# Work moved from VectorE to GpSimd in attention, one multiplication where there were two, and a new order: attention followed by two expert layers on one core

## The chip, the cores and the metric

One core of a Trainium2 chip runs the whole kernel. The metric is device time in microseconds, the median of several executions. Below, TensorE is also PE (its weight loads PEld), VectorE DVE, ScalarE ACT, GpSimd POOL, and the queue that issues most transfers SP.

## The reference

Three stages follow one another, all in fp32:

```
attention: 2 batches x 8 heads, 576 rows, 64 columns a head; x 1152 rows of 512
  scores = q k^T / 8 + (cum[i] - cum[j]), causal;  cum = cumsum(log(clip(f)))
  p = exp(scores - rowmax);  out = (p / (sum(p) + 1e-9)) @ v
layer 1: each row goes to argmax(x @ w_gate + modality_bias[modality_id]) of 8 experts
  out = gate * relu(x w1[e]) w2[e]        (512 -> 1024 -> 512)
layer 2: the same with other weights and no bias; an expert takes at most 288 rows
```

## The kernel before

**Precision by pairs.** Operands of the large matrix products are split into a high part (rounded to fp32r) and a low part (the value less the high part). ACT writes high parts, DVE most low parts. For the weights this is `chunk` (line 364 the high half on ACT, line 373 the low half on DVE), each weight chunk of 128x1024 in two halves of 512 columns.

**A head of attention.** Keys and queries are turned on PE (lines 535, 574, 595) and split (K: L543 on ACT, L547 on DVE, a copy L561 on POOL; Q: L608, L612, L623 likewise; V: L632 on ACT, low part L643 on POOL). Four extra rows, with the cumulated logarithms of f, come from DRAM by a transfer that POOL issues (L1123). Scores are two matmuls and a mask (L675, L676, L679) for each of five tiles of query rows; DVE takes the row maxima (L689), ACT the exponentials with their row sums into `st` (L697). PE turns the exponentials (L715), ACT and DVE split them (L722, L726), and PE multiplies them with V (L748). ACT brings the result to SBUF (L760, L764), and L772 multiplies it with `iw`, which gives for each row 64 output columns and 8 gate logits, side by side in PSUM (72 = NCX columns).

**The end of a head** is what the change touches. On DVE: 1e-9 is added to the row sums (L777) and the reciprocal taken (L780); L785 multiplies the 64 columns by it into `xs`, L789 the 8 logits into `lgh`. After the seventh head of a batch L797 and L800 add the logits of seven heads and the bias, after the eighth L804 adds the last. After each second head SP writes two heads' columns to DRAM (L811 for 512 rows, with 512 bytes a row; L815 for the last 64 rows).

**What follows attention.** While batch 1 is in attention, `early` finds the rows of batch 0 that go to the first expert (L963 to L1019, some thirty small DVE operations in a chain), POOL gathers them (L1025), and the first of that expert's matmuls (`hidden`, L1068) are put between the last heads. For these the first four weight chunks must be split during attention: eight halves, L364 and L373. The buffer that a chunk came in is then loaded with a later chunk (L371, SP).

**What sets the order.** Each operation is handed to a planner (`Sched`) with an engine, an assumed duration and a priority: head number times T plus an offset by kind (`off` in `PAR`; 'N' is the end of a head). The planner writes each engine's fixed program order. Engines take their instructions strictly in that order, so one that waits holds back all behind it on its engine. The split of chunk m has priority (wsp + wsd * m) * T.

Of the kernel before, what the change touches and what calls it, by code (L numbers as in the profile page):

```python
# [8 lines left out]
F32 = mybir.dt.float32  # L9
# [4 lines left out]
ALU = mybir.AluOpType  # L14
AX = mybir.AxisListType
# [3 lines left out]
P = 128  # L19
# [214 lines left out]
def kernel(  # L234
# [17 lines left out]
    par=None,  # L252
):
    nc = tc.nc
    B, H, S, D = q.shape
    N, DM = out.shape
    E = wg1.shape[1]
    BH = B * H
# [18 lines left out]
    psum = actx.enter_context(tc.tile_pool(name="psum", bufs=1, space=PSUM))  # L277

    c_ql_, c_kl_, c_vl_ = ([at.take(sh, F32) for _ in range(n)] for n, sh in ((3, [P, NT, 2, D]), (2, [P, NT, 2, D]), (2, [P, NT, 2, D])))
    iw, xs_ = at.take([P, H, NCX], F32), at.take([P, NT, DM], F32)  # L280
    lf = xs_[0:BH, 0:2].rearrange("p a b -> p (a b)")[:, 0:S]
    nc.sync.dma_start(out=lf, in_=f.rearrange("b h s -> (b h) s"))

    def rows(src, h):
# [60 lines left out]
    def chunk(m, e=None, src=None, raw=None):  # L345

        i, c = divmod(m, NCH)
        rt = RAW[m % NR if raw is None else raw]
        if e is None:
            e, src = expert_of(i)  # L350
        hi, lo = SPL[m % NS] if m % NS < len(SPL) else (None, None)
        if c < KD:
            rv, sv = rt, pick(src[0], e)[c * P:(c + 1) * P, :]
        else:
            k0 = 2 * (c - KD)
            rv = rt.rearrange("p (a d) -> p a d", d=DM)
            sv = pick(src[1], e)[k0 * P:(k0 + 2) * P, :].rearrange("(a p) d -> p a d", p=P)

        def half(t, u):
            return t[:, u * (F1 // 2):(u + 1) * (F1 // 2)]  # L360

        def high(u, eng=None):
            if eng is None:
                nc.scalar.copy(out=half(hi, u), in_=half(rt, u))  # L364
            else:
                eng.tensor_tensor(
                    out=half(hi, u), in0=half(rt, u), in1=one_c.to_broadcast([P, F1 // 2]), op=ALU.mult
                )

        return (  # L370
            lambda: nc.sync.dma_start(out=rv, in_=sv),  # L371
            high,
            lambda u, eng: eng.tensor_tensor(out=half(lo, u), in0=half(rt, u), in1=half(hi, u), op=ALU.subtract),  # L373
        )
# [103 lines left out]
    for t in fresh("ot"):  # L478
        nc.gpsimd.memset(t[:, S:NT * P], 0.0)
    c_rs = slots("rs", [P, NT, 1], F32, 2)  # L480
    lgh = [at.take([P, NT, H, E], F32)] * B
    c_xs = sc.cls("xs", [xs_])

    if not par.get("only"):
# [38 lines left out]
    def head(h, L, G):  # L523
# [243 lines left out]
        def zo():  # L767
            return z.ap[:, HQ:HQ + NT * NCX].rearrange("p (i c) -> p i c", c=NCX)
# [5 lines left out]
        rs = Buf(c_rs)  # L774

        def fn():
            nc.vector.tensor_tensor(  # L777
                out=rs.ap[:, :, 0], in0=st.ap, in1=eps_c.to_broadcast([P, NT]), op=ALU.add
            )
            nc.vector.reciprocal(out=rs.ap, in_=rs.ap)  # L780
        sc.op(D_, 0.17, fn, r=[st], w=[rs], prio=base + O["N"])
        xs = G["xs", b]

        def fn():
            nc.vector.tensor_tensor(  # L785
                out=xs.ap[:, :, hh * D:(hh + 1) * D], in0=zo()[:, :, 0:D],
                in1=rs.ap.to_broadcast([P, NT, D]), op=ALU.mult,
            )
            nc.vector.tensor_tensor(  # L789
                out=lgh[b][:, :, hh, :], in0=zo()[:, :, D:NCX],  # L790
                in1=rs.ap.to_broadcast([P, NT, E]), op=ALU.mult,
            )
        sc.op(D_, 0.5, fn, r=[z, rs], w=[xs, G["lgh"]], prio=base + O["N"])
        lgb = lg[:, 0:E, b * NT:(b + 1) * NT]
        if hh == H - 2:
            def fn():
                nc.vector.tensor_reduce(  # L797
                    out=lgb, in_=lgh[b][:, :, 0:H - 1, :].rearrange("p i h e -> p e i h"), axis=AX.X, op=ALU.add
                )
                nc.vector.tensor_tensor(out=lgb, in0=lgb, in1=btok[:, :, b * NT:(b + 1) * NT], op=ALU.add)  # L800
            sc.op(D_, 0.6, fn, r=[G["lgh"]], w=[G["lg"]], prio=base + O["N"], after=[G["c6"]])
        if hh == H - 1:
            def fn():
                nc.vector.tensor_tensor(  # L804
                    out=lgb, in0=lgb, in1=lgh[b][:, :, H - 1, :].rearrange("p i e -> p e i"), op=ALU.add
                )
            sc.op(D_, 0.12, fn, r=[G["lgh"]], w=[G["lg"]], prio=base + O["N"])
        if hh % 2 == 1:
            def fn():
                c0, t0 = (hh - 1) * D, b * S  # L810
                nc.sync.dma_start(  # L811
                    out=x_d[t0:t0 + KC * P, c0:c0 + 2 * D].rearrange("(i p) d -> p i d", p=P),
                    in_=xs.ap[:, 0:KC, c0:c0 + 2 * D],
                )
                nc.sync.dma_start(  # L815
                    out=x_d[t0 + KC * P:t0 + S, c0:c0 + 2 * D], in_=xs.ap[0:KR, KC, c0:c0 + 2 * D]
                )
            n_ = sc.op("SP", 1.0, fn, r=[xs], prio=base + O["N"], dma=0.83)
            if b == 0:
                G["x0"].append(n_)  # L820

# [276 lines left out]

    a5 = sc.op(D_, 0.2, consts5, prio=par["c5"] * T, after=chain(steps5, par["c5"] * T, [a1, a4]), late=1.0)
    (a6,) = chain(steps6, par["c6"] * T, [a3, a5])  # L1100
    G["c6"], G["lg"], G["lgh"] = a6, Buf(None), Buf(None)
    sc.op("SP", 0.5, zfill2, after=[a3], prio=par["zf"] * T, dma=7.0)
    for b in range(B):
        G["xs", b] = Buf(c_xs)
# [29 lines left out]
    for m in range(NR0):  # L1134
        lb, last, wpr = Buf(None), [], (par["wsp"] + par["wsd"] * m) * T
        sc.op(
            "SP", 0.5, lambda m=m: chunk(m)[0](), w=[lb], after=[a5, a8], dma=1.46, prio=par["w0"] + m * par["w1"],
            late=par["wlate"],
        )
        for u in range(2 if m < KD else 0):  # L1140
            hb = Buf(None)
            if 2 * m + u < par["whp"]:
                sc.op("POOL", 1.2, lambda m=m, u=u: chunk(m)[1](u, nc.gpsimd), r=[lb], w=[hb], prio=wpr + 0.1 * u)
            else:
                sc.op(A_, 0.52, lambda m=m, u=u: chunk(m)[1](u), r=[lb], w=[hb], prio=wpr + 0.1 * u)
            last.append(
                sc.op(D_, 0.61, lambda m=m, u=u: chunk(m)[2](u, vec), r=[hb], w=[wsp[m]], prio=wpr + 0.1 * u)
            )
        if m < KD:
            split_ += last  # L1150
            sc.op("SP", 0.5, lambda m=m: chunk(m + NR)[0](), after=last, dma=1.46, fill=True)
# [1192 lines left out]


PAR = dict(
    wsp=10.0, wsd=0.5528,
    q2n=0, qt=2.7571,
    xprio=4.0,
    te=18.0, dur1=5.6, c5=4.0, c6=5.0, pace=(9.0, 42.0, 2.7),  # L2350
# [3 lines left out]
    marg=0.05, glate=4.0, w2p=1.5, k2e='POOL', ve='ACT', T=7.517, window=29.6757,  # L2354
    w0=54.7241, warm=12, qodd=0.8391, vodd=0.4187, w1=3.4882,
    nbig=2, none=4, pt=[[[0, 0, 576], [3, 384, 576], [4, 512, 576]], [[1, 128, 576]], [[2, 256, 576]]],
    kodd=0.9248, groups=[[4], [3], [2], [0, 1]], off={'aug': -19.3748, 'load': -22.0501, 'T': -13.4108, 'E': -23.4736, 'V': -9.7976, 'S': -5.8296, 'M': -8.5396, 'X': -1.2687, 'PT': -5.0955, 'H': -11.8233, 'AV': 1.8376, 'OT': -16.2636, 'O': 19.7458, 'N': -2.4012}, wf0=6.5, wfd=0.6,
)


# [31 lines left out]
```

## Time and profile before

| what | value |
|---|---|
| median of 3 runs | 469.11 us (468.78 to 472.85) |
| profiled execution | 468.58 us, span 466.8 us |
| PE, PEld busy | 433.5 us (93%), 364.5 us (78%) |
| DVE, ACT, POOL busy | 314.9 us (67%), 270.0 us (58%), 132.0 us (28%) |
| attention's last operation on the logits (L804) | starts at 160.60 us |

A recorded duration includes the time in which an instruction's last results drain, so that back-to-back instructions overlap in the record; a matmul's end is modelled. Idle time is what no recorded instruction covers, with what released the instruction after it. Shares for the whole span mix attention (to about 160 us) with the expert layers.

### The profile page before, as it was taken

The page shows a single profiled execution, that of the slowest core. Times are in us where ns is not written, and L with a number is a line of the kernel's source. Part 1 is how long each engine was busy: PE and PEld are TensorE (multiplying, and loading weights), DVE is VectorE, ACT ScalarE, POOL GpSimd, SP SyncE. Part 2 cuts the span into 40 slices and gives each one's busy share as a digit, 9 for nine tenths or more (in the row PEclk, how much of TensorE's full clock was granted, in tenths as well). Part 3 has the DMA queues.
Part 4 walks back from the last instruction along what each step waited for, and adds up shares of the span by engine and source line. Part 5 has one row for each costly group of instructions (what it writes and reads, how often), then busy time and mean ns, then how long its engine had stood idle before and what let it go on. Part 6 is the DMA issues. An engine that isn't in the chain of part 4 may idle for free. (4 is left out here: it accounts for less than half of the span.)

```text
span 466.8 us, 8038 instructions
## 1 busy us (share of the span) xinstructions
PE 433.5 (93%) x2701; PEld 364.5 (78%) x2701; DVE 314.9 (67%) x717; ACT 270.0 (58%) x603; POOL 132.0 (28%) x171
## 2 busy tenths in 40 slices
PE   7899899898899999999999999989999999999970
PEld 6688787787689978988989877768887778778750
DVE  6787998899985687411952146777849997497330
ACT  6778778799676435202831116356848985597130
POOL 8773344363340013101200010151313344111100
PEclk9999999999999999999999999989999999999996
DMA  6563199994310166501560003349666999460000
GB/s 151 78 145 76 30 157 178 289 289 133 96 67 1 53 207 211 182 24 47 190 217 24 23 24 104 134 125 328 229 208 203 305 322 307 133 210 3 32 4 23
DMA packets 64294, 64.91 MB, mean 139 GB/s; under 512 B 37196, under 2 KB 46412, under 8 KB 64224
## 3 DMA queue, kind: packets, MB, share of 16 engines
q1 hardware_dynamic: 58048, 53.89, 39.7%
q0 software_dynamic: 4992, 10.08, 6.9%
q8 instruction: 25, 0.41, 0.4%
q10 hardware_dynamic: 1200, 0.30, 0.3%
q14 instruction: 29, 0.24, 0.2%
HBM read 56.56 MB, written 11.87 MB: 147 GB/s over the span
## 5 line engine op out<-in xcount | busy, mean ns | idle before, releaser
L2259 POOL DMA_INDIRECT out_dram<-mo,mo x16 | 18.6, 1164 | 104.8 <-DVE mo L2252 83.7
L697 ACT ACTIVATE at<-one,at 128x512 f32<-128x512 f32 (+1 forms) x64 | 33.4, 527 | 9.0 <-DVE at L689 8.6
L748 PE MATMUL one<-at,at 128*128 128x64 f32 (+2 forms) x192 | 35.9, 327 | 2.6 <-ACT at L697 1.5
L2183 ACT ACTIVATE mo<-hps 128x512 f32<-128x512 f32 x30 | 17.7, 606 | 31.0 <-PE hps L2170 18.7
L748 PEld LDWEIGHTS one<-at,at 128*128 128x128 f32 x192 | 28.7, 190 | 5.8 <-ACT at L697 2.2
L2219 PE MATMUL yps<-mo,wb 128*128 128x512 f32 x72 | 29.1, 405 | 0.6 <-PEq L2147 0.3
L689 DVE TENSOR_REDUCE at<-one 128x1 f32<-128x512 f32 (+1 forms) x64 | 28.1, 475 | 0.7 <-PE one L679 0.6
L2221 PE MATMUL yps<-mo,wb 128*128 128x512 f32 x72 | 28.5, 396 | 0.0
L2220 PE MATMUL yps<-mo,wb 128*128 128x512 f32 x72 | 28.5, 396 | 0.0
L1424 POOL DMA_INDIRECT x_d<-mo,mo x8 | 8.1, 1018 | 70.8 <-DVE mo L1421 49.7
L715 PE MATMUL big<-ident,at 128*128 128x128 f32 x128 | 24.3, 274 | 3.8 <-DVE at L547 3.8
L373 DVE TENSOR_TENSOR mo<-wa,mo 128x512 fp32r<-128x512 f32 x42 | 27.3, 682 | 0.7 <-ACT mo L364 0.7
L675 PE MATMUL one<-at,at 128*128 128x512 f32 (+1 forms) x64 | 25.8, 404 | 1.5 <-DVE at L726 1.4
L364 ACT CAST mo<-wa 128x512 fp32r<-128x512 f32 x42 | 24.9, 643 | 0.8 <-DMA wb<-in_moe_w_dram 0.8
L2252 DVE TENSOR_SCALAR mo<-yps,mo 128x512 f32<-128x512 f32 x14 | 10.4, 744 | 21.6 <-PE yps L2221 21.6
L373 DVE TENSOR_TENSOR mo<-wb,mo 128x512 fp32r<-128x512 f32 x36 | 23.7, 684 | 0.5 <-ACT mo L364 0.5
L726 DVE TENSOR_TENSOR at<-one,at 128x320 fp32r<-128x320 f32 (+1 forms) x32 | 17.4, 552 | 9.6 <-ACT at L722 9.4
L715 PE MATMUL one<-ident,at 128*128 128x128 f32 x112 | 22.4, 277 | 1.2 <-ACT at L697 0.6
L373 DVE TENSOR_TENSOR wa<-wb,wa 128x512 fp32r<-128x512 f32 x34 | 21.9, 683 | 2.0 <-ACT wa L364 2.0
L1399 ACT COPY mo<-ytps 128x512 f32<-128x512 f32 (+1 forms) x10 | 5.7, 566 | 30.0 <-PE ytps L1392 30.0
L1268 POOL DMA_INDIRECT wb<-x_d,mo x7 | 7.2, 1023 | 53.4 <-DVE wb L1903 35.9
L364 ACT CAST mo<-wb 128x512 fp32r<-128x512 f32 x36 | 21.4, 636 | 0.8 <-PE yps L2221 0.8
(428 smaller groups left out, 1355.6 us busy)
## 6 DMA issues: line engine op xcount, KB each, us to landing
wb<-in_moe_w_dram SPq DMA_DIRECT2D x35, 512.0 KB, 5.3
wa<-in_moe_w_dram SPq DMA_DIRECT2D x31, 512.0 KB, 5.6
mo<-in_moe_w_dram SPq DMA_DIRECT2D x14, 512.0 KB, 4.4
x_d<-zero SPq DMA_DIRECT2D x1, 2340.0 KB, 18.7
at<-in_k_dram SPq DMA_DIRECT2D x16, 128.0 KB, 2.9
at<-in_q_dram SPq DMA_DIRECT2D x16, 128.0 KB, 2.8
at<-in_v_dram SPq DMA_DIRECT2D x16, 128.0 KB, 2.8
x_d<-at SPq DMA_DIRECT2D x8, 256.0 KB, 2.4
```

Source lines behind the costliest of these rows:

```text
L364: nc.scalar.copy(out=half(hi, u), in_=half(rt, u))
L373: lambda u, eng: eng.tensor_tensor(out=half(lo, u), in0=half(rt, u), in1=half(hi, u), op=ALU.subtract),
L675: nc.tensor.matmul(o, q1.ap[:, s0:s0 + n], k1.ap[:, a:e], start=True, stop=False)
L689: nc.vector.tensor_reduce(out=nm.ap[0:n], in_=ps.ap[0:n, c:c + w], axis=AX.X, op=ALU.max, negate=True)
L697: nc.scalar.activation(out=p.ap[0:n, 0:w], in_=ps.ap[0:n, c:c + w], func=AF.Exp, bias=nm.ap[0:n], scale=1.0, accum_out=st.ap[0:n, i:i + 1],)
L715: nc.tensor.transpose(out=t.ap[:, c:c + P], in_=ptile[i].ap[:, j * P:(j + 1) * P], identity=ident)
L748: nc.tensor.matmul(dst.ap[:, qa - off:qb - off], vt.ap[:, j].rearrange("p a d -> p (a d)"), ph[a][u].ap[:, ca:ca + qb - qa], start=(first ...
L2183: nc.scalar.activation(out=self.s.ap[:, 4 * i:4 * i + 4, :], in_=self.h[i].ap.rearrange("p (c t) -> p c t", t=P), func=AF.Relu,)
L2219: nc.tensor.matmul(self.y.ap, a, wh, start=(c == 0), stop=False)
L2220: nc.tensor.matmul(self.y.ap, a, wl, start=False, stop=False)
L2221: nc.tensor.matmul(self.y.ap, b, wh, start=False, stop=(c == KF - 1))
L2259: nc.gpsimd.indirect_dma_start(out=out, out_offset=blk.at(), in_=o.ap[:, 0:DM], in_offset=None, bounds_check=N - 1, oob_is_err=False,)
```

## The change

It does five things. The low parts of the first four weight chunks (eight halves) are computed by POOL instead of DVE, and their priorities spread from 0.5528 to 0.8093 heads a chunk. Adding 1e-9 to the row sums is an operation of POOL of its own, with a priority 2 us ahead of the reciprocal's, which stays on DVE. `xs` holds 72 columns for each head, so one multiplication over 72 columns takes the place of two over 64 and 8, and `lgh` goes. The write to DRAM after two heads becomes three transfers: one for each head's 512 rows (256 bytes a row) and one for the last 64 rows of both. Five offsets of the plan and `kodd` (the split of the odd head's keys) have other values.

```diff
@@ -277,8 +277,8 @@
     psum = actx.enter_context(tc.tile_pool(name="psum", bufs=1, space=PSUM))
 
     c_ql_, c_kl_, c_vl_ = ([at.take(sh, F32) for _ in range(n)] for n, sh in ((3, [P, NT, 2, D]), (2, [P, NT, 2, D]), (2, [P, NT, 2, D])))
-    iw, xs_ = at.take([P, H, NCX], F32), at.take([P, NT, DM], F32)
-    lf = xs_[0:BH, 0:2].rearrange("p a b -> p (a b)")[:, 0:S]
+    iw, xs_ = at.take([P, H, NCX], F32), at.take([P, NT, H, NCX], F32)
+    lf = xs_[0:BH, 0].rearrange("p a b -> p (a b)")[:, 0:S]
     nc.sync.dma_start(out=lf, in_=f.rearrange("b h s -> (b h) s"))
 
     def rows(src, h):
@@ -478,7 +478,6 @@
     for t in fresh("ot"):
         nc.gpsimd.memset(t[:, S:NT * P], 0.0)
     c_rs = slots("rs", [P, NT, 1], F32, 2)
-    lgh = [at.take([P, NT, H, E], F32)] * B
     c_xs = sc.cls("xs", [xs_])
 
     if not par.get("only"):
@@ -774,48 +773,49 @@
         rs = Buf(c_rs)
 
         def fn():
-            nc.vector.tensor_tensor(
+            nc.gpsimd.tensor_tensor(
                 out=rs.ap[:, :, 0], in0=st.ap, in1=eps_c.to_broadcast([P, NT]), op=ALU.add
             )
+        sc.op("POOL", 0.15, fn, r=[st], w=[rs], prio=base + O["N"] - par["rsp"])
+
+        def fn():
             nc.vector.reciprocal(out=rs.ap, in_=rs.ap)
-        sc.op(D_, 0.17, fn, r=[st], w=[rs], prio=base + O["N"])
+        sc.op(D_, 0.12, fn, w=[rs], prio=base + O["N"])
         xs = G["xs", b]
 
         def fn():
             nc.vector.tensor_tensor(
-                out=xs.ap[:, :, hh * D:(hh + 1) * D], in0=zo()[:, :, 0:D],
-                in1=rs.ap.to_broadcast([P, NT, D]), op=ALU.mult,
+                out=xs.ap[:, :, hh, :], in0=zo(), in1=rs.ap.to_broadcast([P, NT, NCX]), op=ALU.mult
             )
-            nc.vector.tensor_tensor(
-                out=lgh[b][:, :, hh, :], in0=zo()[:, :, D:NCX],
-                in1=rs.ap.to_broadcast([P, NT, E]), op=ALU.mult,
-            )
-        sc.op(D_, 0.5, fn, r=[z, rs], w=[xs, G["lgh"]], prio=base + O["N"])
+        sc.op(D_, 0.45, fn, r=[z, rs], w=[xs], prio=base + O["N"])
         lgb = lg[:, 0:E, b * NT:(b + 1) * NT]
         if hh == H - 2:
             def fn():
                 nc.vector.tensor_reduce(
-                    out=lgb, in_=lgh[b][:, :, 0:H - 1, :].rearrange("p i h e -> p e i h"), axis=AX.X, op=ALU.add
+                    out=lgb, in_=xs.ap[:, :, 0:H - 1, D:NCX].rearrange("p i h e -> p e i h"), axis=AX.X, op=ALU.add
                 )
                 nc.vector.tensor_tensor(out=lgb, in0=lgb, in1=btok[:, :, b * NT:(b + 1) * NT], op=ALU.add)
-            sc.op(D_, 0.6, fn, r=[G["lgh"]], w=[G["lg"]], prio=base + O["N"], after=[G["c6"]])
+            sc.op(D_, 0.6, fn, r=[xs], w=[G["lg"]], prio=base + O["N"], after=[G["c6"]])
         if hh == H - 1:
             def fn():
                 nc.vector.tensor_tensor(
-                    out=lgb, in0=lgb, in1=lgh[b][:, :, H - 1, :].rearrange("p i e -> p e i"), op=ALU.add
+                    out=lgb, in0=lgb, in1=xs.ap[:, :, H - 1, D:NCX].rearrange("p i e -> p e i"), op=ALU.add
                 )
-            sc.op(D_, 0.12, fn, r=[G["lgh"]], w=[G["lg"]], prio=base + O["N"])
+            sc.op(D_, 0.12, fn, r=[xs], w=[G["lg"]], prio=base + O["N"])
         if hh % 2 == 1:
             def fn():
                 c0, t0 = (hh - 1) * D, b * S
+                for u in range(2):
+                    c = c0 + u * D
+                    nc.sync.dma_start(
+                        out=x_d[t0:t0 + KC * P, c:c + D].rearrange("(i p) d -> p i d", p=P),
+                        in_=xs.ap[:, 0:KC, hh - 1 + u, 0:D],
+                    )
                 nc.sync.dma_start(
-                    out=x_d[t0:t0 + KC * P, c0:c0 + 2 * D].rearrange("(i p) d -> p i d", p=P),
-                    in_=xs.ap[:, 0:KC, c0:c0 + 2 * D],
+                    out=x_d[t0 + KC * P:t0 + S, c0:c0 + 2 * D].rearrange("p (r d) -> p r d", d=D),
+                    in_=xs.ap[0:KR, KC, hh - 1:hh + 1, 0:D],
                 )
-                nc.sync.dma_start(
-                    out=x_d[t0 + KC * P:t0 + S, c0:c0 + 2 * D], in_=xs.ap[0:KR, KC, c0:c0 + 2 * D]
-                )
-            n_ = sc.op("SP", 1.0, fn, r=[xs], prio=base + O["N"], dma=0.83)
+            n_ = sc.op("SP", 1.6, fn, r=[xs], prio=base + O["N"], dma=1.0)
             if b == 0:
                 G["x0"].append(n_)
 
@@ -1098,7 +1098,7 @@
 
     a5 = sc.op(D_, 0.2, consts5, prio=par["c5"] * T, after=chain(steps5, par["c5"] * T, [a1, a4]), late=1.0)
     (a6,) = chain(steps6, par["c6"] * T, [a3, a5])
-    G["c6"], G["lg"], G["lgh"] = a6, Buf(None), Buf(None)
+    G["c6"], G["lg"] = a6, Buf(None)
     sc.op("SP", 0.5, zfill2, after=[a3], prio=par["zf"] * T, dma=7.0)
     for b in range(B):
         G["xs", b] = Buf(c_xs)
@@ -1144,7 +1144,9 @@
             else:
                 sc.op(A_, 0.52, lambda m=m, u=u: chunk(m)[1](u), r=[lb], w=[hb], prio=wpr + 0.1 * u)
             last.append(
-                sc.op(D_, 0.61, lambda m=m, u=u: chunk(m)[2](u, vec), r=[hb], w=[wsp[m]], prio=wpr + 0.1 * u)
+                sc.op(
+                    "POOL", 1.25, lambda m=m, u=u: chunk(m)[2](u, nc.gpsimd), r=[hb], w=[wsp[m]], prio=wpr + 0.1 * u
+                )
             )
         if m < KD:
             split_ += last
@@ -2344,7 +2346,8 @@
 
 
 PAR = dict(
-    wsp=10.0, wsd=0.5528,
+    rsp=2.0,
+    wsp=10.0, wsd=0.8093,
     q2n=0, qt=2.7571,
     xprio=4.0,
     te=18.0, dur1=5.6, c5=4.0, c6=5.0, pace=(9.0, 42.0, 2.7),
@@ -2354,7 +2357,7 @@
     marg=0.05, glate=4.0, w2p=1.5, k2e='POOL', ve='ACT', T=7.517, window=29.6757,
     w0=54.7241, warm=12, qodd=0.8391, vodd=0.4187, w1=3.4882,
     nbig=2, none=4, pt=[[[0, 0, 576], [3, 384, 576], [4, 512, 576]], [[1, 128, 576]], [[2, 256, 576]]],
-    kodd=0.9248, groups=[[4], [3], [2], [0, 1]], off={'aug': -19.3748, 'load': -22.0501, 'T': -13.4108, 'E': -23.4736, 'V': -9.7976, 'S': -5.8296, 'M': -8.5396, 'X': -1.2687, 'PT': -5.0955, 'H': -11.8233, 'AV': 1.8376, 'OT': -16.2636, 'O': 19.7458, 'N': -2.4012}, wf0=6.5, wfd=0.6,
+    kodd=1.1276, groups=[[4], [3], [2], [0, 1]], off={'aug': -20.7153, 'load': -22.0501, 'T': -14.5461, 'E': -23.4736, 'V': -9.7976, 'S': -5.8296, 'M': -8.8671, 'X': -1.2687, 'PT': -5.5058, 'H': -11.8233, 'AV': 1.8376, 'OT': -16.2636, 'O': 19.7458, 'N': -2.2729}, wf0=6.5, wfd=0.6,
 )
```

## Rows read from the trace of the kernel before

**Rows 1.** Stretches: us, PE, PEld, DVE, ACT, POOL busy (instructions), clock, DMA, GB/s

```profile
20.00:95.00 75.00, 70.34 (x523) 60.49 (x522) 65.47 (x144) 59.50 (x159) 37.42 (x60) 1.00 0.70 143
95.00:126.00 31.00, 27.66 (x206) 22.31 (x203) 30.54 (x79) 25.98 (x66) 12.56 (x15) 1.00 0.55 167
126.00:141.00 15.00, 14.54 (x111) 12.43 (x110) 13.13 (x27) 12.12 (x33) 6.74 (x8) 1.00 0.28 90
141.00:160.00 19.00, 19.00 (x154) 18.22 (x154) 9.65 (x23) 11.53 (x29) 0.00 (x0) 1.00 0.06 18
```

**Rows 2.** Waits of PE, 95 to 126 us: total us, times, longest

```profile
PE one L675 <- DVE at L726: 1.2, 2, 0.7
PE one L748 <- DVE at L789: 1.1, 1, 1.1
PE big L715 <- DVE at L547: 0.5, 1, 0.5
PE one L715 <- DVE wb L1019: 0.3, 1, 0.3
```

**Rows 3.** Waits of PE, 20 to 95 us

```profile
PE big L715 <- DVE at L547: 3.3, 3, 1.4
```

**Rows 4.** DVE's groups, 95 to 126 us: busy, mean ns, idle before

```profile
L373 DVE TENSOR_TENSOR wa<-wa,wa 128x512 fp32r<-128x512 f32 x8 | 5.9, 740 | 0.0
...
L777 DVE TENSOR_TENSOR at<-at,eps_c 128x5 f32<-128x5 f32 x4 | 0.6, 151 | 0.0
```

**Rows 5.** DVE's groups, 0 to 155 us

```profile
L785 DVE TENSOR_TENSOR at<-one,at 128x320 f32<-128x320 f32 x14 | 6.7, 478 | 0.3 <-PE one L772 0.2
...
L777 DVE TENSOR_TENSOR at<-at,eps_c 128x5 f32<-128x5 f32 x16 | 3.8, 238 | 0.8 <-ACT at L697 0.6
...
L789 DVE TENSOR_TENSOR at<-one,at 128x40 f32<-128x40 f32 x14 | 2.6, 183 | 0.0
```

**Rows 6.** POOL's groups, 95 to 126 us

```profile
L561 POOL TENSOR_TENSOR at<-at,one_c 64x576 fp32r<-64x576 f32 x3 | 3.9, 1323 | 1.9 <-ACT at L543 1.9
L623 POOL TENSOR_TENSOR at<-at,one_c 64x576 fp32r<-64x576 f32 x3 | 3.4, 1142 | 2.4 <-ACT at L608 2.4
L643 POOL TENSOR_TENSOR at<-at,at 128x320 fp32r<-128x320 f32 x3 | 2.6, 881 | 3.7 <-ACT at L632 3.7
```

**Rows 7.** Timeline of DVE: start us, us

```profile
51.78 0.62 DVE L777 TENSOR_TENSOR at<-at,eps_c 128x5 f32<-128x5 f32 x1
...
105.35 0.79 DVE L971 SCALAR_TENSOR_TENSOR wb<-wb 128x40 f32<-128x40 f32 x1
...
124.02 0.69 DVE L373 TENSOR_TENSOR wa<-wa,wa 128x512 fp32r<-128x512 f32 x1
```

**Rows 8.** Timeline of POOL: start us, us, idle before and its releaser

```profile
50.13 2.24 POOL L561 TENSOR_TENSOR at<-at,one_c 64x576 fp32r<-64x576 f32 x2 [2.13 <-ACT at L543]
...
105.22 0.86 POOL L643 TENSOR_TENSOR at<-at,at 128x320 fp32r<-128x320 f32 x1 [0.31 <-ACT at L632]
...
171.52 1.04 POOL L1268 DMA_INDIRECT wb<-x_d,mo  x1 [35.86 <-DVE wb L1903]
```

**Rows 9.** Waits of POOL, 0 to 160 us: total us, times, longest

```profile
POOL at L1123 <- PE one L679: 17.1, 6, 3.3
POOL at L643 <- ACT at L632: 12.3, 9, 3.4
...
POOL wb L1025 <- DVE wb L1019: 4.6, 1, 4.6
```

**Rows 10.** Timeline of PE: the first matmul that needs the eight halves

```profile
143.82 1.43 PE L1068 MATMUL big<-wb,wa 128*128 128x256 f32 x10
```

**Rows 11.** Page, DMA issues: KB each, median us to landing

```profile
at<-in_k_dram SPq DMA_DIRECT2D x16, 128.0 KB, 2.9
...
x_d<-at SPq DMA_DIRECT2D x8, 256.0 KB, 2.4
```

**Rows 12.** Timeline of SP at the end of attention: start us, us

```profile
160.90 0.52 SPq L815 DMA_DIRECT2D x_d<-at  x1
```

## The prediction

> **What bounds the kernel now.** I read the stretches first, because the share of the whole span mixes attention with the expert layers. From 95 to 126 us DVE is busy for 30.54 of 31.00 us: there it is the saturated engine, and PE is idle for 31.00 - 27.66 = 3.34 us. From 20 to 95 us DVE has room (65.47 of 75 us) and PE is idle for 4.66 us. From 126 to 141 us PE lacks 0.46 us, from 141 to 160 us nothing at all [rows 1]. So a change that relieves DVE can pay before 126 us, and behind 141 us PE itself is the limit: what comes out of attention earlier moves the rest of the kernel forward by as much, because the expert layers have no instruction of the change in them.
>
> The second view is what PE waited for. From 95 to 126 us it is DVE each time: 1.2 us for low parts of the exponentials, 1.1 us for the logits' multiplication (it frees the PSUM tile), 0.5 us for low parts of K, 0.3 us for the early route, 3.1 us in all of the 3.34 [rows 2]. From 20 to 95 us it is 3.3 us for low parts of K [rows 3]. The reader is to see that 3.1 + 3.3 = 6.4 us is about all that a faster DVE can give back. A little more hides behind the drain that a record includes, so I let the ceiling be 8 us.
>
> **The change part by part: what DVE loses.** The eight low halves take 740 ns each, 8 x 0.740 = 5.9 us, all of it in the saturated stretch [rows 4]. Adding 1e-9 takes 16 x 0.238 = 3.8 us over the span, though only 4 x 0.151 = 0.6 us in the stretch [rows 4, 5]. The second multiplication, 183 ns for 40 columns, becomes 40 more columns of the first. At the first one's 478 / 320 = 1.5 ns a column that is 0.06 us, so each head saves 0.183 - 0.06 = 0.12 us, 16 x 0.12 = 2.0 us over the span and 0.4 us in the stretch (three heads) [rows 5]. Sum: 5.9 + 3.8 + 2.0 = 11.7 us over attention, 5.9 + 0.6 + 0.4 = 6.9 us in the stretch.
>
> **What POOL gains.** The trace has no fp32 subtraction of 512 columns on POOL. The nearest is the low part of V, two inputs from SBUF, 881 ns for 320 columns; in proportion that gives 881 x 512 / 320 = 1.41 us. The other end follows from the slope to the copies of 576 columns (1142 ns): 881 + 192 x (1142 - 881) / 256 = 1.08 us [rows 6]. I take 1.25 us, between the two, since the operation is the nearer one in kind and the width lies between: 8 x 1.25 = 10 us, with 8.6 and 11.3 as ends. Adding 1e-9 to five columns isn't there either: not under DVE's 0.15, not over the 0.88 of 320 columns [rows 4, 6]; I take 0.2, near the short end, 16 x 0.2 = 3.2 us. POOL is busy for 12.56 of 31 us in the stretch [rows 1]; with some 7 us of the halves (the last two chunks are now planned later) and 0.8 us of additions it comes to 20, so it has the time. The halves' consumer is the first early matmul at 143.82 us [rows 10]; the last half now starts at 124.02 us [rows 7]. Chunk 3 is put off by 3 x (0.8093 - 0.5528) = 0.77 heads of about 9 us, to about 131 us, which leaves 11 us of cover. If that cover goes, PE waits at 143.82 for what is missing.
>
> **What the port costs.** POOL and DVE stand in each other's way here: the addition at 51.78 us took 0.62 us where its kind takes 0.15, and ended at 52.40, just when POOL's copies of 50.13 to 52.37 had ended; a small operation of the early route at 105.35 took 0.79 us and ended with POOL's 105.22 to 106.08 [rows 4, 7, 8]. So the change takes victims away (additions, halves) and leaves about ten operations of the early route with two SBUF inputs. POOL's SBUF work covers 3.9 + 3.4 + 2.6 = 9.9 us of the 31, about 0.32 [rows 6]; 7 us more make it 0.55. Ten operations x 0.23 more chance x half of 1.25 us is 1.4 us that DVE gives back. Ends: 0 (none is hit) and 10 x 0.62 = 6.2 us (each is).
>
> **Moved and added waits.** POOL's queue is long on waits: 17.1 us in six waits before the transfers of the four rows, 12.3 us in nine before V's low parts, 4.6 us before the early gather [rows 9]. Whatever stands behind them (the halves, the additions) is late with them, and behind a half of 1.25 us the copies of K and Q and the four rows' transfers start later in turn; they are made about a head ahead, which hides most of it. I charge 0.5 us, with 0 and 3 as ends (a wait of a copy's length, 1.14 us, some three times). The reciprocal now waits for POOL; behind it on DVE stand the next head's maxima and low parts, for which ACT and PE wait. That is the rival below.
>
> **The transfers.** SP issues one transfer more for each pair of heads: 0.4 us, which matters only where something queues behind it. Two of 128 KB with short rows land in about 2.9 us like the loads of K, where 256 KB took 2.4 [rows 11]. The last pair was issued by 160.90 + 0.52 us [rows 12]; landing at 163 it becomes 164 to 164.5. The first reader is the gather at 171.52 us, released by DVE [rows 8]: 7 us of cover, so I cost it at nothing; the ends are 0 and 1 us. The Trainium skill, "DMA: Bandwidth & Descriptors", Specifications, puts the least size for full rate at 512 bytes and has the engines read, modify and write below it, which speaks against this part; by it the sum would still be the same, since the cover is longer than twice the old landing time.
>
> **The sum.** In the stretch DVE is relieved of 6.9 - 1.4 = 5.5 us, more than the 3.1 us that PE waited for it. I take 2.8 of these, because relieved waits partly pass to ACT. Before 95 us DVE loses about 8 x (0.238 + 0.12) = 2.9 us, where it isn't saturated; of the 3.3 us I take a third, 1.1. Less 0.5 for POOL's queue: 2.8 + 1.1 - 0.5 = 3.4 us. The profiled execution took 468.58 us, 0.5 below the median, and would become 465.2; against the median the forecast is 469.11 - 3.4 = **465.7 us**. The new offsets only permute the order; I give them 0, with 2 us either way.
>
> **The rivals.** (a) More comes back: the new order also removes most of the waits on K's low parts (transposes are planned 1.1 us earlier), and the whole 6.4 us and the drains go: -7, 462. For it speaks that these waits are few and long (1.4 us [rows 3]), against it that DVE has room there and they are matters of order. (b) The port takes it back: every one of the ten operations meets a half, 6.2 us, so that 6.9 - 6.2 = 0.7 us is left, time 468.5. The additions and the operation of 105.35 show that the mechanism exists. The Trainium skill, "SBUF — State Buffer", Who interferes with whom, says that a DVE instruction with two SBUF inputs and a GpSimd instruction that reads SBUF exclude each other for the whole instruction; the trace agrees with it at 0.79 and 0.62 us. (c) The saturation moves: ACT, busy 25.98 of 31 us [rows 1], becomes what PE waits for, and nothing is gained, 469. (d) **Slower**: the reciprocal stands on DVE behind an addition that POOL reaches late. Its place is each head's end, its price POOL's mean wait, 12.3 / 9 = 1.4 us, or 17.1 / 6 = 2.9 us [rows 9]. Five heads of 16 at 1.4 us are 7 us of DVE's stall: 469.1 - 3.4 + 7 = 472.7. It decides once the stalls exceed 3.4 us. Against it: the addition is ready when ACT's sums are, POOL's idle time is larger than its work, and the plan has these waits in it; for it: the plan's durations aren't the chip's, and DVE's order is fixed.
>
> **How the numbers follow.** About 1% (4.7 us) is what a measurement of this kernel can tell from no change. My forecast holds 0.45 (gain of 1.5 to 5.5, of which 0.11 is beyond 1%), (a) 0.2, (b) 0.09, (c) 0.09, (d) 0.17 (0.11 of it beyond 1%). Faster: 0.2 + 0.11 = 0.31; slower 0.11; same 0.58. The range from 461.5 (most of (a)) to 471.5 (a part of (d), the upper ends of port and queue) leaves out some 0.07 below and 0.12 above.
>
> **What would show it.** Right: eight halves on POOL at 1.1 to 1.4 us; one multiplication a head at about 0.53 us; DVE's share well under 0.95 in the stretch; PE's waits on DVE there under 1 us; L804's place at about 157 us instead of 160.6, and from there to the end the same length to within 0.7 us. Wrong: a total of DVE's waits on POOL at the reciprocal of over 2 us (d), early-route operations of 0.7 us and more in number (b), ACT as the releaser of PE's waits (c), or a gain that arises behind 160 us.

## The result: slower by 1.0%, where a gain of 0.7% was forecast

The changed kernel takes 474.09 us (median of 6 runs, 473.11 to 475.89), the kernel before beside it 468.94 us; ratio 1.0104, 95% interval 1.0072 to 1.0137. The profiled execution took 473.55 us with a span of 471.8 us. The forecast was 465.7 us, the range ended at 471.5: the prediction was wrong in sign.

**Where the time went.** The first view is the stretches of the changed kernel, with the columns of [rows 1].

```profile
20.00:95.00 75.00, 71.58 (x534) 61.60 (x534) 63.98 (x132) 61.47 (x164) 40.85 (x79) 1.00 0.72 142
95.00:126.00 31.00, 26.28 (x161) 22.35 (x160) 26.16 (x47) 20.72 (x52) 18.96 (x20) 0.83 0.63 175
126.00:141.00 15.00, 13.62 (x96) 12.22 (x95) 11.75 (x26) 11.45 (x30) 8.10 (x10) 0.77 0.27 79
```

To 95 us it went as forecast: PE is idle for 3.42 us instead of 4.66. From 95 to 126 us DVE is no longer saturated (26.16 of 31 us against 30.54), and still PE does less: 161 matmuls against 206, idle 4.72 us against 3.34, at a mean clock of 0.83. Attention's last operation on the logits (now L801) starts at 166.68 us against 160.60, so the loss of 6.1 us arises between 95 and 141 us; from there to the issue of the last store it takes 1.6 us less than before (292.9 against 294.5 us), and the kernel before had a stretch of 3.4 us at half clock near 307 us that is missing here.

**What held DVE up.** The next two fences are timelines of DVE and of POOL in the changed kernel (start us, us, engine, line).

```profile
94.86 0.86 DVE L965 TENSOR_TENSOR wb<-lg,wb 128x40 f32<-128x40 f32 x1
95.76 1.25 DVE L968 TENSOR_TENSOR_SCAN wb<-rste,wb 128x40 f32<-128x40 f32 x1
97.05 1.15 DVE L971 SCALAR_TENSOR_TENSOR wb<-wb 128x40 f32<-128x40 f32 x1
...
105.79 1.09 DVE L976 CAST wb<-wb 128x5 bf16<-128x5 f32 x1
...
106.87 1.12 DVE L979 TENSOR_SCALAR wb<-wb 128x5 f32<-128x5 f32 x1
...
119.01 0.61 DVE L994 TENSOR_TENSOR wb<-wb 128x5 f32<-128x5 f32 x1
...
121.14 2.77 DVE L995 TENSOR_SCALAR wb<-wb 128x5 f32<-128x5 f32 x1
...
125.40 0.89 DVE L999 TENSOR_SCALAR wb<-iota_b,wb 128x128 bf16<-128x128 bf16 x5
...
126.48 1.15 DVE L1003 TENSOR_TENSOR wb<-iota_c,wb 128x10 bf16<-128x10 f32 x1
```

```profile
94.80 0.87 POOL L642 TENSOR_TENSOR at<-at,at 128x320 fp32r<-128x320 f32 x1
95.63 2.50 POOL L373 TENSOR_TENSOR wa<-wa,wa 128x512 fp32r<-128x512 f32 x2
...
105.71 2.24 POOL L560 TENSOR_TENSOR at<-at,one_c 64x576 fp32r<-64x576 f32 x2
...
117.07 2.52 POOL L373 TENSOR_TENSOR wa<-wa,wa 128x512 fp32r<-128x512 f32 x2
...
121.39 2.49 POOL L373 TENSOR_TENSOR wa<-wa,wa 128x512 fp32r<-128x512 f32 x2
...
126.46 1.14 POOL L560 TENSOR_TENSOR at<-at,one_c 64x576 fp32r<-64x576 f32 x1 [2.59 <-ACT at L542]
```

The reader is to lay one on the other. L965 ends at 95.72, after V's low part (94.80 to 95.67); L968 and L971 end at 97.01 and 98.20 with the two halves (95.63 to 98.13); L976 and L979 share the two copies of 105.71 to 107.95; L994 ends at 119.62, after the halves of 117.07 to 119.59; L995, an operation on five columns that took 0.16 us before, stands for 2.77 us, until both halves of 121.39 to 123.88 are through; and L1003 ends with the copy of 126.46. The kernel before shows it less: L971 takes 0.79 us [rows 7], L968 0.48 us, and L999 needs 1.95 us for four operations, where the changed kernel needs 0.89 us for five. Timeline of DVE before:

```profile
96.92 0.48 DVE L968 TENSOR_TENSOR_SCAN wb<-rste,wb 128x40 f32<-128x40 f32 x1
...
117.11 0.16 DVE L995 TENSOR_SCALAR wb<-wb 128x5 f32<-128x5 f32 x1
...
119.31 1.95 DVE L999 TENSOR_SCALAR wb<-iota_b,wb 128x128 bf16<-128x128 bf16 x4
```

**What PE made of it.** Timeline of PE in the changed kernel; brackets give the idle time before an instruction and what ended it.

```profile
98.78 0.33 PE L674 MATMUL one<-at,at 128*128 128x128 f32 x1 [2.10 <-DVE at L725]
...
99.56 2.36 PE L771 MATMUL one<-at,at 128*128 128x72 f32 x10
...
111.26 1.29 PE L771 MATMUL one<-at,at 128*128 128x72 f32 x10
...
125.36 1.32 PE L747 MATMUL one<-at,at 128*128 128x64 f32 x8 [2.44 <-ACT at L696]
...
128.09 0.46 PE L1016 MATMUL one<-wb,wb 128*128 128x2 bf16 x10 [1.38 <-DVE wb L1006]
```

Behind L971 stood the low parts that free a PSUM bank, so PE idled for 2.10 us; behind L995 stood a maximum, behind that an exponential (ACT then waited 3.23 us for DVE), and PE idled for 2.44 us; then it idled for 1.38 us for L1006, which stood behind L1003. After the idle times of 2.10 and 2.44 us the granted clock is at the lower of its levels. Stretches of the changed kernel again:

```profile
99.40:109.60 10.20, 10.20 (x43) 9.24 (x42) 7.96 (x16) 5.95 (x17) 3.62 (x5) 0.50 0.98 276
109.60:126.70 17.10, 14.48 (x111) 12.14 (x110) 14.57 (x31) 13.79 (x34) 12.45 (x14) 1.00 0.36 101
126.70:133.50 6.80, 5.42 (x32) 5.14 (x30) 4.87 (x10) 4.09 (x12) 4.03 (x5) 0.50 0.30 77
```

At 1.2 GHz the ten matmuls of L771 took 2.36 us, at 2.4 GHz 1.29. Here lies a trap of the page: from 99.4 to 109.6 us PE counts as busy without a break, because each of its 43 instructions takes longer. In its profiled execution the kernel before had the clock at 1.00 throughout attention [rows 1].

**What the change says it does, it does.** Groups of the changed kernel: two of DVE from 0 to 155 us, then two of POOL from 95 to 126 us (busy us, mean ns, idle before).

```profile
L787 DVE TENSOR_TENSOR at<-one,at 128x360 f32<-128x360 f32 x13 | 6.8, 522 | 0.9 <-PE one L771 0.6
...
L782 DVE RECIPROCAL at<-at 128x5 f32<-128x5 f32 x15 | 2.7, 182 | 1.4 <-POOL at L776 1.3
```

```profile
L373 POOL TENSOR_TENSOR wa<-wa,wa 128x512 fp32r<-128x512 f32 x8 | 10.0, 1274 | 0.8 <-ACT wa L364 0.8
...
L776 POOL TENSOR_TENSOR at<-at,eps_c 128x5 f32<-128x5 f32 x2 | 0.4, 190 | 5.1 <-ACT at L696 5.0
```

### The profile page after: what moved, and what is told of

Read it like the earlier page. It is cut to its first block, busy times and chain, and to the rows that moved or that the text cites. A ratio compares the mean times of both kernels' runs of the same rounds, so it can differ in the third digit from the quotient of the medians.

```text
span 471.8 us, 8056 instructions
## 1 busy us (share of the span) xinstructions
PE 437.4 (93%) x2700; PEld 369.5 (78%) x2700; DVE 313.0 (66%) x677; ACT 270.0 (57%) x603; POOL 145.1 (31%) x195
## 5 line engine op out<-in xcount | busy, mean ns | idle before, releaser
L747 PE MATMUL one<-at,at 128*128 128x64 f32 (+2 forms) x192 | 37.6, 340 | 2.8 <-ACT at L696 2.8
L747 PEld LDWEIGHTS one<-at,at 128*128 128x128 f32 x192 | 30.2, 202 | 5.8 <-ACT at L696 3.1
L560 POOL TENSOR_TENSOR at<-at,one_c 64x576 fp32r<-64x576 f32 x16 | 18.2, 1142 | 10.6 <-ACT at L542 10.5
```

The costliest lines, as they stand in the source:

```text
L560: nc.gpsimd.tensor_tensor(out=kk2.ap[0:D, 1], in0=kk1.ap[0:D, :], in1=one_c[0:D, :].to_broadcast([D, S]), op=ALU.mult,)
L747: nc.tensor.matmul(dst.ap[:, qa - off:qb - off], vt.ap[:, j].rearrange("p a d -> p (a d)"), ph[a][u].ap[:, ca:ca + qb - qa], start=(first ...
```

## The experiments

My theory after the result: POOL's halves and the early route's chain (L963 to L1019) meet in time, DVE's small operations wait until POOL's are through, PE idles, and its clock falls. The rivals: the new order as such, POOL's time as such, the reciprocal's wait for POOL's addition, the transfers.

**1. Halves on DVE, plan unchanged.**

```diff
-    "POOL", 1.25, lambda m=m, u=u: chunk(m)[2](u, nc.gpsimd), ...
+    "POOL", 1.25, lambda m=m, u=u: chunk(m)[2](u, vec), ...
```

> The changed kernel with its plan as it is; only the eight low halves are executed by DVE at the places where the plan had POOL do them. Theory 1 (port and clock): in the changed kernel the early route's operations L965, L968, L971 and L995 took 0.86, 1.25, 1.15 and 2.77 us because POOL read SBUF at the same time, PE then idled for 2.1 and 2.4 us, and each time its clock was halved afterwards (10.2 and 6.8 us at 1.2 GHz). Without POOL's halves L965 to L971 are back at 0.2 to 0.5 us, both stretches at half clock are gone, and the time is 467 to 470 us. Theory 2 (the new order is bad by itself): the waits of PE near 97 and 123 us stay and the time stays at 472 to 475.

Measured: 471.66 us, ratio 1.0052 (1.0023 to 1.0081). L968 and L971 are back at 0.23 and 0.20 us, L995 at 0.15. L979 took 1.94 us beside POOL's copies of K, and two stretches at half clock are left (6.8 us from 108, 3.4 us from 129). Half of the loss is gone, and the time lies between the ranges of the two theories. What is left in the profile is the meeting with POOL's older work: L965 (0.85 us) and L976 (0.98 us) still stand beside it, and L979 waits through a copy and V's low part. Whether that is all that is left isn't shown.

**2. Halves as fills.**

```diff
-    "POOL", 1.25, lambda m=m, u=u: chunk(m)[2](u, nc.gpsimd), ...
+    "POOL", 1.25, lambda m=m, u=u: nc.gpsimd.memset(SPL[m][1][:, u * 512:(u + 1) * 512].bitcast(F32), 0.0), ...
```

> The changed kernel with its plan as it is, but POOL writes zeros to the eight low halves and reads nothing (these low parts are left out of the first expert's first matmuls). POOL stays busy for about 0.5 us a half at the same places. Theory 1 (POOL's reading of SBUF is what holds DVE up): L965 to L971 at 0.2 to 0.5 us, L995 at 0.15, no half clock near 100 and 127 us, total 464 to 468 us. Theory 2 (order): 472 to 475 us. If the halves hurt only by occupying POOL's queue, something between, as 0.5 us a half are left of 1.25.

Measured: 470.36 us, ratio 1.0024 (1.0002 to 1.0047). Timeline of DVE, then of POOL:

```profile
95.71 0.24 DVE L968 TENSOR_TENSOR_SCAN wb<-rste,wb 128x40 f32<-128x40 f32 x1
95.98 0.20 DVE L971 SCALAR_TENSOR_TENSOR wb<-wb 128x40 f32<-128x40 f32 x1
...
103.11 2.86 DVE L979 TENSOR_SCALAR wb<-wb 128x5 f32<-128x5 f32 x1
```

```profile
95.56 0.99 POOL L1148 MEMSET wa<- 128x512 f32 x2
...
101.95 2.24 POOL L560 TENSOR_TENSOR at<-at,one_c 64x576 fp32r<-64x576 f32 x2
104.16 0.85 POOL L642 TENSOR_TENSOR at<-at,at 128x320 fp32r<-128x320 f32 x1
104.96 0.98 POOL L1148 MEMSET wa<- 128x512 f32 x2
```

L968 and L971 ran in the middle of POOL's fills and weren't slowed: it is POOL's reading that held them, as theory 1 says. L979, which has one input and a constant, waited even through the second pair of fills, to 105.97 us. PE then idled for 2.55 us and ran 10.2 us at half clock, which is my account of why the time stayed above the 464 to 468 us that theory 1 expected.

**3. The 72 columns alone.** `fused_only` is the changed kernel with the halves and the 1e-9 back on DVE and `PAR` as before.

> The kernel before with one part of the change alone: one multiplication over 72 columns, xs with 72 columns a head, three transfers for a pair of heads. Low halves and the 1e-9 stay on DVE, plan values as before. DVE loses 16 x 0.12 = 2 us. Theory 1: this part costs nothing, so 466.5 to 469.5 us, no half clock in attention. If the transfers with 256-byte rows or the wider multiplication were at fault: 471 or more.

Measured: 467.87 us, ratio 0.9979 (0.9953 to 1.0005). A second time, in another set:

> The 72-column multiplication alone once more, with more rounds, beside the last version: 466.5 to 469 us; a ratio of 0.995 to 1.000 if its 2 us less on DVE are worth anything.

Measured: 467.89 us, ratio 0.9979 (0.9952 to 1.0007). The multiplication and the three transfers cost nothing; that they gain can't be told from no change.

**4. DVE held up on purpose, in the kernel before.**

```diff
+    for _ in range(5):
+        vec.memset(W["xg"][0], 0.0)
     vec.scalar_tensor_tensor(out=U["cn"], in0=U["cn"], scalar=1.0, in1=U["eq"], ...)    # L971
```

> The kernel before, its plan unchanged, with five fills of 520 columns on DVE put ahead of the early route's L971 (near 105 us), which hold DVE for some 1.5 to 3 us where it is saturated. The price of one late DVE. If only the wait counts (rival): the time rises by no more than DVE is held, 470 to 472 us. Theory 1: PE idles for some 2 us, its clock is at 1.2 GHz for several us afterwards, and the time rises by clearly more than DVE is held, 473 to 477 us.

Measured: 476.47 us, ratio 1.0165 (1.0127 to 1.0203), 7.5 us more. The fills held DVE from 107.76 to 110.83 us, 3.1 us, and two operations behind them then met POOL's copies (1.51 and 1.14 us). The wait of PE, and the stretch after it:

```profile
114.52 0.69 PE L675 MATMUL one<-at,at 128*128 128x384 f32 x1 [4.84 <-DVE at L726]
```

```profile
113.00:125.00 12.00, 10.48 (x49) 9.09 (x50) 9.45 (x24) 5.44 (x16) 0.99 (x2) 0.57 0.24 71
```

Not all of the 7.5 us is the price of the fills. In the profiled execution a stretch at half clock at the start (10.2 us from 11.5), which the profile of the kernel before lacks, has already put the chain's first operation (L963) back by 2.3 us (98.30 against 96.03). From there to the last operation on the logits it loses another 7.1 us (71.67 against 64.57), more than twice the 3.1 us for which the fills held DVE. PE idles 3.6 us more in that time (7.38 against 3.80), so by this reckoning 3.5 us are left for the 10.2 us at half clock from 113.8.

**5. The idle places filled.** PE repeats score matmuls at head 10 (three times) and 13 (twice), and does five matmuls into a bank ahead of L1016.

```diff
+    one_s, again = fn, {(10, 2): 4, (13, 4): 3}.get((h, g[-1]), 1)
+    def fn(one_s=one_s, again=again):
+        for _ in range(again):
+            one_s()
     sc.op("PE", d, fn, r=[q1, k1, qk2], w=[ps], prio=base + O["S"])
...
```

> The changed kernel, plan and data as they are, with more work for PE: in the three places where it idled (2.1 us at 97, 2.4 us at 123, 1.4 us at 127 us) it first repeats the score matmuls that it has just done (three times 0.65 us and twice 0.95 us, into the same tiles with the same values) or does five matmuls of 512 columns into a bank that it is about to use. If the idle gaps bring the clock down (theory 1), the stretches at half clock of 10.2 and 6.8 us shrink or go, and the time falls from 474 to 468 to 471 us although PE has 5 us more to do. If only the waits count, the time stays at 474 or rises to 476.

Measured: 475.14 us, ratio 1.0119 (1.0075 to 1.0162). Timeline of PE:

```profile
98.66 0.33 PE L674 MATMUL one<-at,at 128*128 128x128 f32 x1 [0.67 <-DVE at L730]
...
99.38 1.29 PE L776 MATMUL one<-at,at 128*128 128x72 f32 x10
...
107.87 1.60 PE L719 MATMUL big<-ident,at 128*128 128x128 f32 x8 [1.69 <-DVE at L546]
```

The mechanism showed and the time did not follow. Both old stretches at half clock are gone (ten matmuls in 1.29 us where they took 2.36), but PE, now faster, ran into the next hold-up (L979's counterpart, 1.94 us beside a copy and V's low part), idled for 1.69 us and ran 10.2 us at half clock from there. The expectation of 468 to 471 us was a miss: keeping PE busy at some holes doesn't help while DVE is late at others.

**6. The change without the halves.** Low halves back on DVE in the plan too (`wsd` 0.5528), everything else as changed.

> The change without its first part: low halves on DVE as before (also in the plan, spread 0.5528), 1e-9 on POOL, 72 columns at once, new offsets. If POOL's halves are what costs (theory 1): 466 to 469 us, L965 to L995 mostly under 0.5 us, no half clock in attention. If the new offsets, which put L965 and L979 next to POOL's copies of K and Q, cost by themselves (theory 2; the last runs with halves on DVE or as fills kept one or two stretches at half clock): 470 to 473 us with a wait of DVE at L979 or L965 of 0.9 us or more.

Measured: 468.66 us, ratio 0.9989 (0.9956 to 1.0022): the loss is gone in the median. The profiled execution, at 472.26 us the slowest of the ten, shows that the meeting doesn't need the halves on POOL: there a half on DVE stands for 2.46 us beside two copies and V's low part, PE idles for 1.97 us, and a stretch of 10.2 us at half clock begins at 105.5 us, which theory 1 did not expect.

**7. The halves on POOL with the old offsets** (`off` and `kodd` as before).

> The change with the offsets and kodd of before: POOL still computes the halves (spread 0.8093) and adds 1e-9, 72 columns at once. With the runs so far this completes a square: halves on POOL or DVE, new or old offsets (POOL, new: 474.1; DVE, new: 468.7; DVE, old: 467.9). Theory 1 (the halves meet the early route's chain at SBUF's port, whatever the offsets): several operations of L965 to L1006 over 0.8 us, at least one stretch at half clock, 470.5 to 475 us. Theory 2 (it takes the new offsets too): 467 to 470 us.

Measured: 475.94 us, ratio 1.0167 (1.0117 to 1.0217). L968 1.25 us, L971 1.15, L995 and L997 1.20 each; half clock for 3.4 us from 100 and 13.7 us from 120. With runs 3 and 6 the square is full: halves on POOL 474.1 and 475.9, on DVE 468.7 and 467.9. With the halves at these places of the plan their engine decides, the offsets don't. The square isn't quite clean: with the halves on DVE their spread is 0.5528 too, and run 3 has the addition of 1e-9 on DVE; run 8 has that part alone.

**8. 1e-9 on DVE, plan unchanged.**

```diff
-    nc.gpsimd.tensor_tensor(out=rs.ap[:, :, 0], in0=st.ap, in1=eps_c.to_broadcast([P, NT]), op=ALU.add)
+    pass        # and the same addition by nc.vector, ahead of the reciprocal
```

> The changed kernel, plan as it is, with the addition of 1e-9 executed by DVE just ahead of the reciprocal instead of by POOL. In the changed kernel DVE waited for POOL's addition 1.3 us in all. My theory: this part is not the cause, so 472.5 to 476 us, the halves still in the way. If DVE's wait for POOL were the cause (the rival that I called slower): 470 us or less.

Measured: 474.52 us, ratio 1.0107 (1.0072 to 1.0143). L995 still stands there for 2.89 us. My slower rival isn't the cause.

**9. Halves on POOL, earlier.** `wsp` 8.4, `wsd` 0.35, `wlate` 4.

> The whole change with POOL doing the halves, but planned earlier (from head 8.4, spread 0.35, loads taken as landed after 4 us instead of 10), so that all eight are done before the early route's chain begins. Theory 1 (halves and chain meet at SBUF's port): the long durations of L965 to L995 go, 465 to 469 us. Theory 2 (order and other copies): a wait on POOL's copies stays, 470 to 473 us.

Measured: 470.58 us, ratio 1.0030 (1.0000 to 1.0060). Above the 465 to 469 us of theory 1 and inconclusive as a test: the long durations went but for one of 1.27 us, but the halves waited 6.2 us for their high parts, which wait for the loads; PE idled for 1.82 and 3.25 us near 85 and 89 us, and the stretch at half clock now lies there.

**10. Two versions with less on DVE.** `no_eps_fused` drops the addition and takes the reciprocal of the sums; `early_lows_dve` also plans the halves on DVE from head 8.4.

```diff
-    nc.vector.reciprocal(out=rs.ap, in_=rs.ap)
+    nc.vector.reciprocal(out=rs.ap[:, :, 0], in_=st.ap)
```

> The kernel before with the 72-column multiplication and without the addition of 1e-9 at all: a row's sum holds the exponential of its maximum, so it is at least 1, and 1e-9 added to it is lost in fp32; the reciprocal reads the sums directly. Halves on DVE, offsets as before. DVE loses 3.8 + 2.0 = 5.8 us against the kernel before, without a new instruction on POOL. Theory 1: 465 to 468 us, no half clock in attention; if every new order of the plan is a lottery, 470 or more.

Measured: 468.14 us, ratio 0.9989 (0.9963 to 1.0014). Another 3.8 us off DVE, and no gain that can be told. The profile has one stretch at half clock in attention (3.4 us from 121.9), where theory 1 expected none.

> A version meant to be faster than both: no addition of 1e-9 (lost in fp32 beside a sum of at least 1), 72 columns at once, halves on DVE but planned from head 8.4 on (spread 0.35, loads taken as landed after 4 us), which takes them out of the stretch in which DVE is saturated. Offsets as before. If DVE's saturation from 95 to 126 us is worth its 3.1 us of waits: 464 to 467 us. If a late load or a new gap of PE before 95 us takes its place: 468 to 471.

Measured: 477.27 us, ratio 1.0179 (1.0137 to 1.0221), the slowest of all and outside both ranges. DVE's timeline shows why: a half in fixed order, waiting for a high part whose load hadn't come; PE idled for 4.25 us, and its clock was halved from 84.9 us on.

```profile
83.42 0.69 DVE L373 TENSOR_TENSOR wa<-wa,wa 128x512 fp32r<-128x512 f32 x1 [4.70 <-ACT wa L364]
```

**11. Halves on POOL, after the chain.** Two numbers of the change: `wsp` 13.2 instead of 10.0, `wsd` 0.25 instead of 0.8093; with the new offsets, then with the old ones.

> The whole change, with the halves on POOL planned later (from head 13.2, spread 0.25), so that they run after the early route's chain (L963 to L1019), when few operations with two inputs from SBUF are left on DVE. Theory 1 (the meeting is the cause): no operation of the chain over 1 us because of a half, the stretches at half clock near 99 and 127 us go or shrink, 466 to 469.5 us. Rival (POOL's time as such, or a late half before the first early matmul): 471 to 475 us.

> The same with the offsets and kodd of before (halves on POOL after the chain, 1e-9 on POOL, 72 columns at once). Theory 1: 465.5 to 469 us, against 475.9 with the halves beside the chain. Rival: 471 or more.

Measured: **463.68 us, ratio 0.9889 (0.9866 to 0.9913)**, and 464.38 us, ratio 0.9897 (0.9864 to 0.9929). The first, by view: stretches, then POOL's halves, then DVE's chain.

```profile
95.00:126.00 31.00, 28.62 (x224) 24.24 (x222) 27.63 (x67) 24.01 (x62) 14.66 (x19) 1.00 0.51 142
126.00:141.00 15.00, 14.40 (x103) 12.05 (x104) 9.93 (x20) 14.34 (x39) 13.05 (x13) 1.00 0.47 118
```

```profile
128.16 5.04 POOL L373 TENSOR_TENSOR wa<-wa,wa 128x512 fp32r<-128x512 f32 x4
...
133.98 3.77 POOL L373 TENSOR_TENSOR wa<-wa,wa 128x512 fp32r<-128x512 f32 x3
```

```profile
96.06 0.23 DVE L968 TENSOR_TENSOR_SCAN wb<-rste,wb 128x40 f32<-128x40 f32 x1
...
99.82 0.18 DVE L971 SCALAR_TENSOR_TENSOR wb<-wb 128x40 f32<-128x40 f32 x1
...
102.10 1.12 DVE L979 TENSOR_SCALAR wb<-wb 128x5 f32<-128x5 f32 x1
...
115.10 0.15 DVE L995 TENSOR_SCALAR wb<-wb 128x5 f32<-128x5 f32 x1
```

The same halves on the same engine with the same 10 us now cost nothing that can be seen: PE is idle for 2.38 us from 95 to 126 us (before: 3.34), does 224 matmuls there instead of 206, and its clock stays up. That POOL's time as such was the cost is excluded. What is left of the meeting is L965 (0.86 us) and L979 beside POOL's older work. Both times lie below the ranges that theory 1 gave, which I can't account for in full. This version beats both kernels, and two numbers separate it from the changed one.

## Why the prediction was wrong

**What was right.** DVE is relieved as worked out: a 72-column multiplication takes 522 ns (478 + 60 forecast), a half on POOL 1274 ns (1.25 us), an addition there 190 ns (0.2). From 20 to 95 us PE's idle time fell by 1.24 us (1.1), its waits on K's low parts from 3.3 to 1.6 us; with 1e-9 back on DVE (run 8) the early route starts at 96.15 us instead of 94.06. The transfers are free: the first gather after attention, at 177.72 us, is still released by DVE, not by them. POOL's queue does not hold up the reciprocal: 1.3 us in two waits over all heads, so rival (d), the only slower one that I had, is refuted by the profile and by run 8. A gain exists too: 3.4 us were promised, and the change with its halves moved behind the chain gains 1.1%, some 5 us (469.0 x 0.0111 = 5.2). That doesn't prove the forecast's sum: the median clock is 0.989 there against 0.981 in the kernel before beside it, and by the slope given below some 1.9 us of the gain go with that.

**The step that failed is "What the port costs".** "Ten operations x 0.23 more chance x half of 1.25 us is 1.4 us", with 6.2 us as the upper end. Against the 0.15 to 0.24 us that they take when free (in the kernel before, in run 2 or in the fastest version), L965, L968, L971, L976, L979, L994, L995 and L1003 lost 0.64 + 1.01 + 0.97 + 0.94 + 0.97 + 0.45 + 2.62 + 1.00 = 8.6 us. In the kernel before the chain lost 2.1 us (L968 0.24, L971 0.61, L999 1.30), so the change added 6.5 us where I had 1.4, above the upper end. Of the 8.6 us 5.0 fall to the halves (L968, L971, L994, L995); the other 3.6 were lost beside copies of K and V's low part, which the kernel before has too and which the chain now meets at other points. I had put the new order at nothing; without the halves beside the chain (runs 6 and 11) it costs nothing that can be told. Three assumptions were off:
- The victims. I counted operations with two inputs from SBUF. L976, L979 and L995 have one input, and lost 4.5 of the 8.6 us.
- The length. I took half of one operation. L968, L971, L976 and L979 each waited through about a whole one (0.94 to 1.01 us), L995 through a pair of halves (2.6 us), and L979 in run 2 through copies, V's low part and fills (2.7 us).
- The chance. I spread POOL's work evenly and had 7 us of the halves in the stretch. All eight ran there, 10.0 us, and three of the four pairs, at 95.6, 117.1 and 121.4 us, right beside the chain. The plan prices neither engine with the other's presence, so nothing kept them apart.

**The step that was missing is the clock.** I reckoned a wait of DVE as at most its own length, for PE to lose. Two idle times of PE of 2.10 and 2.44 us (with 1.38 behind it) were followed by 10.2 and 6.8 us at 1.2 GHz. The sum in the profiled execution: PE idles 2.3 us more from 95 to 141 us (6.10 against 3.80) and 1.6 us less before; the start of L801 is 6.1 us later; so 6.1 - 2.3 + 1.6 = 5.4 us are left for the clock, which is less than half of 17 us, as it must be. PE had as much to do up to there (1092 matmuls against 1094). How often the clock falls differs between executions. Over the 84 executions of the kernel before in the sets of runs 1 to 11, 0.01 less of mean clock goes with 2.4 us more; its median is 0.982, the changed kernel's 0.969, which makes some 3 of the 5.1 us between the medians. That slope holds the idle times that come with the falls as well. In run 4 the same sum left 3.5 of 7.1 us for the clock. So the clock is about half of the loss or more; this split is reckoned, not shown by an experiment, since filling the holes (run 5) only moved them.

**Rival (b) was the right mechanism at the wrong size**, put at "0.7 us is left" where it cost 1%. My own sign for it came: seven operations of the early route of 0.7 us and more. The rule of the Trainium skill that I set beside it ("SBUF — State Buffer", Who interferes with whom) holds here at more points than I used. The Trainium skill says there that a DVE instruction with two SBUF inputs contends with a GpSimd instruction that reads SBUF, not with one that only writes it. The trace agrees: L968 and L971 took 0.24 and 0.20 us amid POOL's fills, 1.25 and 1.15 amid its halves. The Trainium skill also says there that copies, casts and `tensor_scalar` can, under conditions on their operands, enter modes in which they contend with GpSimd for the shared port pair. The trace agrees as far as it goes: L976, L979 and L995 are a cast and two `tensor_scalar`, and L979 waited through fills as well (2.86 us); no run shows the mode itself. The prediction used the first rule and left the second out.

**The one rival that ended slower** (472.7 us) came near the measured time by a mechanism that isn't there.

## What to carry to other kernels

In this kernel, work moved from VectorE to GpSimd paid only where it didn't run beside a chain of small VectorE operations that read SBUF: check the target stretch for casts, `tensor_scalar` and two-input operations before moving, and let the plan keep the two apart (here two numbers turned +1.0% into -1.1%). Less work on VectorE alone gave nothing that can be told (runs 3 and 10). Price a late engine by what stands behind it, and where TensorE would idle for some microseconds, add a stretch at half clock to the price. When a profile after shows less load on the engine that was saturated and yet more time, look at the granted clock by stretch first.

## What the runs showed of the hardware that was not expected

- A VectorE operation on five columns (0.16 us when free) can stand for 2.77 us: L995 of the changed kernel didn't get in between two GpSimd operations that followed each other without a break. That isn't always so: L968 and L976 there (1.25 and 1.09 us), and L995 in run 7 (1.20 us), got in after the first of two.
- Fills by GpSimd (writing only) let two-input VectorE operations through (0.24 and 0.20 us in run 2), but not the one `tensor_scalar` that met them behind other GpSimd work (2.86 us).
- TensorE's clock fell to 1.2 GHz at idle times of 2.10 us (the changed kernel), 2.55 us (run 2) and 1.69 us (run 5) inside otherwise busy stretches, and stayed there for 10.2 us each time; behind the 2.44 us of the changed kernel it stayed there for 6.8 us. The length of the idle time alone doesn't settle it: the clock stayed up after 1.85 us near 9 us of the changed kernel and of the fastest version, and of two idle times that ended near 55.7 us, 1.67 us in run 7 and 1.68 us in run 11 with the old offsets, only the second was followed by a fall (6.8 us from 57.4).
